# A fused attention and FFN kernel: its hand-kept order of 1,427 work items is replaced by another order

## The chip, the cores and the metric

The kernel runs on one core of a Trainium2 chip. The metric is the device time of one execution in microseconds (us). The engines are TensorE (PE; its weight loads are told as PEld), VectorE (DVE), ScalarE (ACT), GpSimd (POOL) and SyncE (SP). SP only issues transfers here; POOL issues the loads that cast from float32 to bfloat16 on their way, and computes as well. Each engine takes its own instructions in the order in which they were written.

## The reference

```python
def _attn_ref(q, k, v, w_phi):          # q, k, v: (8, 8, 576, 64); w_phi: (64, 128)
    def phi(x):
        proj = np.einsum('bhsd,df->bhsf', x, w_phi)
        proj = proj - np.max(np.abs(proj), axis=-1, keepdims=True)
        return np.concatenate([np.exp(proj), np.exp(-proj)], axis=-1)
    q_p, k_p = (phi(q), phi(k))
    kv = np.einsum('bhsf,bhsd->bhfd', k_p, v)
    z = np.sum(k_p, axis=2)
    num = np.einsum('bhsf,bhfd->bhsd', q_p, kv)
    den = np.einsum('bhsf,bhf->bhs', q_p, z)[..., None] + 1e-06
    return num / den
def _moe_ref(x, w_gate, w_val, w_out):  # x: (4608, 512); d_ff = 1536
    gate = np.maximum(x @ w_gate, 0.0)
    val = x @ w_val
    return gate * val @ w_out
```

The output of the attention, with heads side by side, is x of the FFN. All inputs and the output are float32.

## The kernel before

There are 8 batches of 576 tokens. Of a batch, 512 tokens are one group of the FFN (groups 0 to 7), and the last 64 tokens of all batches ("tails", taken two batches at a time) make group 8. Batches 0 and 1 are turned (tokens to columns) by TensorE; from batch 2 on (`TURN = 2`) k, q and x are turned by DMA, on SP's queue.

The program is cut into 1,427 work items ("atoms"). A planner outside the kernel has put them into one list, the string `ORDER`; the kernel walks the list and lets each atom issue its instructions. An apostrophe behind a number takes the atom's second choice of engine (ACT or DVE for a copy, POOL or DVE for a product). `z5` issues 5 filler matmuls on zeros, which only keep TensorE busy. The list sets the order on each engine and in each queue: an instruction that must wait holds up all that stands behind it on its engine. What waits for what follows from the tiles. PSUM is a ring of 8 banks, so a matmul group also waits for the readers of the bank eight allocations ahead of it.

Atoms are named here by their kind and place, with batch, item, half and so on behind it:

- `ld.k6`, `ld.q1`, `ld.v4`, `ld.wv1`, `ld.km3`, `ld.qm0`: loads. Those of k, q and the weights cast and are issued by POOL (`L214`, `L220`, `L236`, `L243`); those of v are float32 and are issued by SP. `km`, `qm` and `vm` are the tails. A batch's k, q and tails have one buffer each, v has two.
- `turn.k.2`, `turn.qm.0`: turns of k, q or tails by DMA from SP (`L292`, `L298`). `xd.3.2`: the turn of the third quarter of x of batch 3 by DMA from SP (`L639`), into `xT`; batch "8" there is the tails.
- Work on k: `kT`, `kTc` (turn on PE and its copy, `L271`, `L284`; batches 0 and 1), `kr` (projection, PE, `L312`), `km` (row maxima, DVE, `L319`), `ke` (two exponentials, ACT, `L368`), `kk` (exponentials of the maxima, ACT, `L379`), `vs` (v times these, POOL or DVE, `L328`, `L410`), `kv` (PE, `L482`; `L505` for batches 0 and 1, 72 matmuls), `kvc` (its copy, `L418`).
- Work on q: `qT`, `qTc`, `qr`, `qm`, `qc` (PE, `L543`), `qe` (ACT, `L561`), `qk` (ACT, `L577`), `n` (PE, `L591`), `nt` and `nu` (DVE, `L610`, `L622`), `xu` (reciprocal on DVE, product on POOL, `L629`, `L631`), then `xd`, or for batches 0 and 1 `xT` and its copy `xc` (`L651`).
- FFN: `fv`, `fg` (four matmuls each, `L721`; the copy of `fv` is `L736`, the product of `fg` `L743`), `fo` (four matmuls, `L769`; every third one also copies and stores its result, `L783`, `L750`).

The loads of k and v of batch 0 and the constants stand ahead of the list and are the same in both kernels.

Of the kernel before, what the change touches and what calls it, by code (L numbers as in the profile page):

```python
# [22 lines left out]

ORDER = """z5 92 82 83' 93 7 94 97 102 84 98 88 8 95 99 0 103 85 87 89 86 104 105 96 112 107 109 122 113 123
108 114 115 106 117 124 127 100 90 132 133 101 91 110 126 125 119 118 128 111 z3 148 129 149 116
187 188 134 135 137 151 156 153 155 158 120 121 142 144' 160 143' 1 139 10 138 246 247 150 131 196
198 154 130 157 159 152 161 141 136 200 140 29 175 190 189 194 162 176 193 192 163 164 145 147' 195
191 236 165 177 2 146 169 199 170 166 167 181 171 178 168 321 179 201 172 182 217 197 180 237' 322'  # L30
183 184 220 266 267' 282 9 218 214 215 3 221 219 222 4 216 223 256 257' 173 174' 226 208 185 186
209 54 283' 202 203 238 242 210 205 206 227 204 207 211 1092 241 1093 240 1094 1095 1096 1097 224
225' 239 1098 212 213' 324 326 228 229 232 5 1099 231 1100 11 39 230 328 1101 1102 233 1103 1104'
1105 1106 1107 234 258 268 269 262 259 270 260 271 273 261 263 6 272 248 249 275 251 253 255 243
1108 1109 1110 1111 1112' 1113 250 252 1114 1115 284 254 288 330 334 264 286 361 365 332 274 1116
1117 335 290 292 363 265 279 280' 323 325 285 327 289 1118' 1119 287 294 245 235 1120 244 291 293
295 281 276 360 329 277 331 278 296 1121 13 1122' 30 1123 333 31 14 303 304 1124 342 305 300 301
# [3 lines left out]
1134 358 359' 398 401 402 58 61 388 1135 1136 392 389 60 1137 1138 32 391 399 403 59 63 1139 414  # L41
415 1140' 400 1141 367 368 1142 390 1143 15 393 42 373 369 374 375 62 1144 1145 1146 1147 384 1148
419 421 395 64 418 394 422 425 427 429 1149 1150 423 396 397 430 1151 420 17 43 454 458 456 424 385
426 386 387' 416 417' 404 405 406 428 459 407 463 460 462 464 461 465 453 65 431 432 433 1152 437
438 445 446 457 1153 455 434 435 436 1154' 448 449 1155 439 440 441 1156 450 447 442 1157 443 444
472 473 451 452 33 1158' 469 470 483 477 478 1159 1160 466 479 1161 1162 1163 484 485 480 534 471
467 468 474 475 481 476 508 482 486 538 498 501 20 487 509 536 376 1164 1165' 502 1166 511 535 537
539 529 533 500 513 510 512 1167 1168 1169 518 522 499 515 519 531 528 564 568 503 520 1170 530 505
52 55 504 521 18 514 540 1171 1172' 566 1173 569 488 492 489 1174' 491 573 1175 493 494 532 523 524
1176' 377 495 1177 1178' 516 571 1179 1180' 490 496 497 517 570 66 69 563 565 506 567 1181 1182 34  # L50
# [4 lines left out]
585 1200 616 586 617 646 650 618 657 23 647 661 620 649 651 653 1201' 659 648 1202 1203 608 1204  # L55
1205 691 609 610 626 627 695 693 619 621 21 629 631 628 22 46 56 663 665 623 630 667 1206 633 1207
1208' 1209 642 1210' 662 666 656 692 694 696 658 660 622 664 1211 1212' 644 645' 624 625 632 634
635' 698 702 697 701 699 736 739 1213 672 700 652 1214 1215 1216 1217 654 668 740 718 673 737 669
670 703 671 738 741 742 655 1218' 1219 1220 675 707 676 721 614 722 674 680 677 1221 1222 715 678
681 682 679 708 709 1223 723 615 716 717 1224 686 719 720 687 688 1225 1226 1227 1228 683 684 746  # L60
749 724 748 756 685 747 758 766 1229 768 1230' 1231 704 705 1232 706 760 36 710 711 1233 689 47 750
757 690 770 751 752 712 759 725 713 714 1234 802 804 743 726 728 773 730 727 761 762 729 777 775
1235 1236 25 1237 1238 1239 806 767 771 26 769 731 772 774 801 53 805 776 1240' 778 49 1241 753 754
755' 803 1242 837 841 807 809 733 732 808 810 1243' 1244' 811 744 763 764 745 765 734 735 24 1245
785 779 812 782 783 784 780 781 839 813 1246 1247 796 1248' 814 815 1249 37 820 821 822 816 1250
1251 786 787 817 818 819 823 824 1252 1253 1254 74 797 78 798 836 788 75 840 1255 838 1256' 76 1257
77 790 791 48 792 1258 846 842 847 825 826 828 1259 1260' 829 830 848 827 789 1261 1262 793 831 832
794 795 1263 849 850 851 1264 1265 1266 1267 1268 864 38 833 834 835 866 854 858 884 885 886 867
865 799 856 800 1269 1270' 1271 1272 868 1273 1274 857 855 859 874 869 887 870 877 900 902 878 876
79 894 80 1275 1276 1277 896 1278 875 860 1279' 1280' 898 1281 888 843 904 844 879 881 845 1282  # L70
1283 901 27 903 895 899 861 929 897 931 1284' 1285 933 1286 905 1287 930 889 964 966 932 967 935
939 965 937 968 871 1288' 872 880 882 883 28 50 873' 934 890 1289 862 863 891 892 893' 994 936 940
938 906 941 974 977 1290 1291 907 908 909 975 996 1292 1293 978 910 911 912 979 980 976 995 913 914
852 969 970 915 916 1294 57 997 1295 1296 998 921 853 917 956 957 922 999 1001 918 919 942 943 958
1297 1298 1299 1300 923 944 924 925 926 948 81 949 950 1301 1302' 1303 920 945 946 947 951 952 1000
1304 984 988 927 928 1046 1048 971 987 1004 1006 1305 953 1306 1307 1050 959 985 989 960 1002 1003
1008 1308 954 955 986 961 962 963 1309' 1310 972 973' 1005 1009 1007 981 1010 1014 1012 1040 1044
1042 1311 1312 1051 1039 1011 1043 1045 1047 1013 982 1313 983' 1041 1314 1315' 1316' 1317 1318
1028 1015 1016 1029 1052 1053 1054 1034 1035 1036 1058 1059 1049 1060 991 1319 1320 1321 990 1322
1323 1324 1325 992 993' 1030 1326' 1327 1069 1070 1063 1064 1071 1031 1328' 1329 1065 1055 1056  # L80
# [6 lines left out]
1404 1405 1406 1407 1408 1409 1410 1411 1412 1413 1414 1415 1416 1417 1418 1419 1420' 1421 1422  # L87
1423 1424 1425 1426'"""


class Atoms:
# [28 lines left out]
def kernel(  # L120
# [690 lines left out]

    atoms.run(ORDER, keep_busy)
# [28 lines left out]
```

## Time and profile before

| | us |
|---|---|
| median of 3 runs | 383.99 |
| lowest, highest | 382.81, 384.39 |
| profiled execution | 383.07 |
| its span | 381.3 |
| TensorE busy | 366.9 |
| VectorE busy | 280.2 |
| ScalarE busy | 221.9 |
| GpSimd busy | 153.4 |

The span runs from the first to the last instruction of the profiled execution; the time of the execution has 1.8 us more. Busy times are sums over the span. They hide where an engine waits, so they have to be read by stretches: the attention of batches 0 and 1 fills the first 32 us, from there to about 310 us the attention of one batch runs beside the FFN of earlier ones, and the FFN of the last groups fills the rest.

### The profile page before, as it was taken

How to read it: one execution, taken by the hardware profiler on the slowest of the kernel's cores; microseconds unless marked ns; L12 is line 12 of the kernel's file. 1: busy time of each engine (PE TensorE's matmuls, PEld its weight loads, DVE VectorE, ACT ScalarE, POOL GpSimd, SP SyncE). 2: the span in 40 equal slices, each digit the busy share in tenths (PEclk: the TensorE clock that was granted, in tenths of full speed). 3: DMA queues.
4: the chain of work that ended last, by engine and by line, in shares of the span. 5: the costliest groups of instructions: out<-in, count | busy, mean ns of one | idle time of the engine just before them, and what ended most of it. 6: DMA issues, size and time to landing. Idle time of an engine off the chain costs nothing.

```text
span 381.3 us, 8930 instructions
## 1 busy us (share of the span) xinstructions
PE 366.9 (96%) x3454; PEld 199.0 (52%) x3504; DVE 280.2 (73%) x617; ACT 221.9 (58%) x521; POOL 153.4 (40%) x203
## 2 busy tenths in 40 slices
PE   6979999999999999899999999999999999999996
PEld 3658555546544655365546454555555444444443
DVE  6889888888988799779877984999767905845421
ACT  5889887788388657774972549783751413200221
POOL 5856672568356365713680314816800400100000
PEclk9989999999999999999999999999999999999999
DMA  7999999799399827961698903671310150001004
GB/s 238 233 232 165 179 177 161 185 209 204 70 134 254 100 55 133 221 141 34 85 166 164 214 15 107 152 114 29 98 55 2 28 113 28 15 36 74 2 2 108
DMA packets 87929, 45.10 MB, mean 118 GB/s; under 512 B 55824, under 2 KB 82000, under 8 KB 87888
## 3 DMA queue, kind: packets, MB, share of 16 engines
q1 hardware_dynamic: 60208, 30.42, 35.0%
q0 software_dynamic: 27200, 13.57, 29.0%
q10 hardware_dynamic: 480, 0.56, 0.6%
q8 instruction: 27, 0.44, 0.5%
q14 instruction: 14, 0.11, 0.1%
HBM read 37.78 MB, written 9.44 MB: 124 GB/s over the span
## 4 chain that ended last, share of the span: by engine, by line
PE 88%; DMA 4%; ACT 3%; issue 2%; DVE 1%; POOL 1%; SPq 0%; DVEq 0%; POOLq 0%
PE pa L721 49%; PE pa L769 22%; PE pa L591 5%; PE pa L312 4%; PE pa L482 4%; PE pa L543 2%; DMA xT<-xu 2%; DMA vn<-in_k_dram 2%; ACT kp L368 1%; PE pa L505 1%; PE pa L271 1%; ACT qp L561 1%; ACT tT L284 1%; SPq L220 0%; POOL xu L631 0%
## 5 line engine op out<-in xcount | busy, mean ns | idle before, releaser
L743 DVE SCALAR_TENSOR_TENSOR h<-pa,val_sb 128x512 bf16<-128x512 f32 (+1 forms) x112 | 74.4, 669 | 35.0 <-PE pa L721 30.1
L721 PE MATMUL pa<-xT,wv_sb 128*128 128x512 bf16 (+1 forms) x384 | 97.8, 370 | 2.1 <-DMA xT<-xu 1.0
L721 PE MATMUL pa<-xT,wg_sb 128*128 128x512 bf16 (+1 forms) x384 | 98.0, 370 | 0.8
L769 PE MATMUL pa<-wo_sb,h 128*128 128x512 bf16 (+2 forms) x428 | 96.9, 373 | 1.5 <-issue 1.0
L736 ACT CAST val_sb<-pa 128x512 bf16<-128x512 f32 (+1 forms) x75 | 42.8, 575 | 85.5 <-PE pa L721 82.7
L328 POOL TENSOR_TENSOR vs<-vn,ek 128x512 bf16<-128x512 f32 (+1 forms) x70 | 69.3, 1000 | 44.6 <-ACT ek L379 39.9
L561 ACT ACTIVATE qp<-pa 128x512 bf16<-128x512 f32 x144 | 75.7, 619 | 16.8 <-PE pa L543 14.6
L368 ACT ACTIVATE kp<-pa 128x512 bf16<-128x512 f32 (+1 forms) x152 | 77.6, 601 | 12.2 <-PE pa L312 10.4
L631 POOL TENSOR_TENSOR xu<-u,r 128x512 bf16<-128x512 f32 x36 | 37.4, 1043 | 115.1 <-DVE r L629 79.5
L721 PEld LDWEIGHTS <-wv_sb 128*128 128x128 bf16 x448 | 41.5, 98 | 45.0 <-PE pa L769 1.5
L769 PEld LDWEIGHTS <-h 128*128 128x128 bf16 x444 | 41.0, 98 | 45.7 <-issue 1.1
L721 PEld LDWEIGHTS <-wg_sb 128*128 128x128 bf16 x448 | 41.4, 98 | 43.4 <-issue 0.7
L319 DVE TENSOR_REDUCE mk<-pa 128x4 f32<-128x512 f32 (+1 forms) x76 | 47.4, 651 | 8.3 <-PE pa L312 4.2
L319 DVE TENSOR_REDUCE mq<-pa 128x4 f32<-128x512 f32 x72 | 46.6, 681 | 3.3 <-PE pa L312 2.9
L610 DVE TENSOR_TENSOR t<-pa,cq 128x195 f32<-128x195 f32 (+3 forms) x120 | 37.8, 328 | 4.1 <-PE pa L591 3.1
L622 DVE TENSOR_TENSOR u<-pa,t 128x195 f32<-128x195 f32 (+3 forms) x120 | 38.1, 332 | 3.4
L591 PEld LDWEIGHTS <-qp 128*128 128x128 bf16 x640 | 28.4, 98 | 14.0 <-issue 0.9
L736 DVE CAST val_sb<-pa 128x512 bf16<-128x512 f32 (+1 forms) x37 | 25.1, 678 | 12.0 <-PE pa L721 11.2
L591 PE MATMUL pa<-kv,qp 128*128 128x65 bf16 x640 | 31.1, 194 | 0.4 <-ACT qp L561 0.2
L783 ACT COPY out_sb<-pa 128x512 f32<-128x512 f32 (+1 forms) x22 | 13.1, 594 | 26.2 <-PE pa L769 25.8
L783 DVE COPY out_sb<-pa 128x512 f32<-128x512 f32 x14 | 9.6, 687 | 21.0 <-PE pa L769 20.8
L482 PEld LDWEIGHTS <-kp 128*128 128x128 bf16 x480 | 16.5, 98 | 3.6 <-issue 0.8
(66 smaller groups left out, 265.8 us busy)
## 6 DMA issues: line engine op xcount, KB each, us to landing
out_dram<-out_sb SPq DMA_DIRECT2D x32, 256.0 KB, 2.5
vn<-in_v_dram SPq DMA_DIRECT2D x6, 1024.0 KB, 7.8
qn<-in_q_dram POOLq DMA_DIRECT2D x8, 512.0 KB, 8.8
kn<-in_k_dram POOLq DMA_DIRECT2D x6, 512.0 KB, 8.6
wv_sb<-in_moe_w_val_dram POOLq DMA_DIRECT2D x3, 512.0 KB, 10.1
wg_sb<-in_moe_w_gate_dram POOLq DMA_DIRECT2D x3, 512.0 KB, 8.8
wo_sb<-in_moe_w_out_dram POOLq DMA_DIRECT2D x1, 1536.0 KB, 14.7
vn<-in_v_dram SPq DMA_DIRECT2D x1, 1152.0 KB, 10.4
```

Of the source, the lines that this page charges most:

```text
L319: nc.vector.tensor_reduce(m, some.rearrange("p (c f) -> p c f", f=F), axis=AX.X, op=ALU.max, apply_absolute_value=True,)
L328: eng.tensor_tensor(dst[:, :, s, 0:D], src, ek[:, :, s : s + 1].to_broadcast(list(src.shape)), op=ALU.mult,)
L368: nc.scalar.activation(st["kp"][:, s, 0 : n // 2, par, :], st["banks"][par][:, 0 : n // 2 * F].rearrange("p (a f) -> p a f", f=F), AF.Exp, ...
L561: nc.scalar.activation(x["qp"][:, s, slot].rearrange("p a b -> p (a b)"), st["cols", i][par], AF.Exp, scale=sign,)
L591: nc.tensor.matmul(pn[:, E * (2 * i + s) : E * (2 * i + s + 1)], lhsT=x["qp"][:, s, slot, blk, :], rhs=kv_of(b, lo + i)[:, s, :],)
L610: nc.vector.tensor_tensor(x["t", j][rows, 0:n], ab[:, :, 1], c[:, :, None].to_broadcast([np_, n, E]), op=ALU.mult,)
L622: nc.vector.tensor_tensor(x["u"][rows, lo : lo + n], ab[:, :, 0], x["t", j][rows, 0:n], op=ALU.add)
L631: copy_of(alt, nc.gpsimd, nc.vector).tensor_tensor(x["xu"], x["u"][:, :, 0:D], x["r"].to_broadcast([P, H, D]), op=ALU.mult)
L721: nc.tensor.matmul(ps, lhsT=w[:, dc, P * fi : P * fi + P], rhs=xTs[g][:, dc, lo:hi], start=(dc == 0), stop=(dc == NDC - 1),)
L736: copy_by(copy_of(alt, "ACT", "DVE"))(st["val", n], ps)
L743: nc.vector.scalar_tensor_tensor(st["h2"][:, fi, lo:hi], ps, 0.0, st["val", n], op0=ALU.max, op1=ALU.mult)
L769: nc.tensor.matmul(po, lhsT=st["h2"][:, fi, P * t : P * t + P], rhs=wo_sb[:, fi, c0:c1], start=(fi == 0), stop=(fi == NFC - 1),)
```

## The change

Only `ORDER` is replaced. The atoms, their code and their number are the same; both lists hold each of them once. Filler matmuls go from `z5` and `z3` to `z3` and `z1`. Two atoms of `vs` go from POOL to DVE. Of the copies, 14 `kvc` on DVE become 15, 37 `fv` become 33, 15 `fo` become 14; 4 `kTc` on ACT become 7, 2 `qTc` become 1, 6 `xc` become 5. All else is place. The words of the change say that the planner now charges an order for transfers that other transfers push back, and keeps the turns of x by DMA clear of casting loads.

The diff is too long to show whole (some 63 lines out and in). Its head, and the lines that hold the last turn of x for batch 3 (atom 586) and the load of k for batch 6 (atom 23):

```diff
-ORDER = """z5 92 82 83' 93 7 94 97 102 84 98 88 8 95 99 0 103 85 87 89 86 104 105 96 112 107 109 122 113 123
-108 114 115 106 117 124 127 100 90 132 133 101 91 110 126 125 119 118 128 111 z3 148 129 149 116
-187 188 134 135 137 151 156 153 155 158 120 121 142 144' 160 143' 1 139 10 138 246 247 150 131 196
...
-585 1200 616 586 617 646 650 618 657 23 647 661 620 649 651 653 1201' 659 648 1202 1203 608 1204
...
+ORDER = """7 z3 82 83' 92 93' 84 88 87 85 8 94 98 96 97 89 91' 95 102 103' 0 z1 104 105 99 107 112 122 113 114
+86 106 109 108 123 124 90' 117 116 128 1 132 100 115 148 110 125 119 133' 127 118 101 187 134 111
+120 121 129 149 151 188 131 10 126 155 153 156 160 246 130 157 142 137 158 135 139 141 247' 159 161
...
+1193 1194 584 1195 1196 605 604 611 34 606 607 576 1197 638 577 643 578 585 586 1198 1199 1200 657
...
+725 675 676 709 677 672 673 1224 1225 674 1226 683 684 685 746 766 749 756 757 23 770 678 679 750
...
```

Places in the two lists (counted from 0) of atoms that the text speaks of:

| atom | number | before | after |
|---|---|---|---|
| `vs.0.0.1`, on POOL before, on DVE after | 91 | 42 | 16 |
| `km.0.1.0` | 95 | 13 | 17 |
| `kk.0.1` | 99 | 14 | 24 |
| `ld.q1` | 10 | 73 | 62 |
| `ld.wv1` | 2 | 109 | 86 |
| `ld.qm0` | 29 | 91 | 99 |
| `turn.qm.0` | 54 | 156 | 100 |
| `ld.v1` | 9 | 136 | 107 |
| `qT.1.1`, the first user of `ld.q1` | 321 | 120 | 141 |
| `xT.0.1`, `xc.0.1` (on DVE before, on ACT after) | 185, 186 | 153, 154 | 149, 155 |
| `fv.0.0`, the first step of the FFN | 1092 | 169 | 171 |
| `vs.1.0.0`, the first user of `ld.v1` | 234 | 204 | 200 |
| `xd.2.2` | 476 | 513 | 531 |
| `ld.v4` | 18 | 560 | 545 |
| `fv.2.0` | 1172 | 564 | 579 |
| `ld.km3` | 36 | 855 | 650 |
| `xd.3.2` | 586 | 702 | 694 |
| `ld.k6` | 23 | 708 | 836 |
| `xd.4.0` | 679 | 817 | 839 |
| `ld.q5` | 22 | 736 | 744 |
| `fv.3.0` | 1208 | 747 | 739 |

More of the change, by code (lines that the diff above doesn't have):

```diff
@@ L22 @@
 LAST = ((0, 352), (352, 512))
-ORDER = """z5 92 82 83' 93 7 94 97 102 84 98 88 8 95 99 0 103 85 87 89 86 104 105 96 112 107 109 122 113 123
-108 114 115 106 117 124 127 100 90 132 133 101 91 110 126 125 119 118 128 111 z3 148 129 149 116
-187 188 134 135 137 151 156 153 155 158 120 121 142 144' 160 143' 1 139 10 138 246 247 150 131 196
-198 154 130 157 159 152 161 141 136 200 140 29 175 190 189 194 162 176 193 192 163 164 145 147' 195
-191 236 165 177 2 146 169 199 170 166 167 181 171 178 168 321 179 201 172 182 217 197 180 237' 322'
@@ L31 @@
[L31 to L36, printed above, removed]
@@ L37 @@
-295 281 276 360 329 277 331 278 296 1121 13 1122' 30 1123 333 31 14 303 304 1124 342 305 300 301
[3 rows of a table removed]
[L41 to L50, printed above, removed]
[4 rows of a table removed]
@@ L55 @@
-585 1200 616 586 617 646 650 618 657 23 647 661 620 649 651 653 1201' 659 648 1202 1203 608 1204
[L56 to L77, printed above, removed]
@@ L78 @@
-1042 1311 1312 1051 1039 1011 1043 1045 1047 1013 982 1313 983' 1041 1314 1315' 1316' 1317 1318
-1028 1015 1016 1029 1052 1053 1054 1034 1035 1036 1058 1059 1049 1060 991 1319 1320 1321 990 1322
-1323 1324 1325 992 993' 1030 1326' 1327 1069 1070 1063 1064 1071 1031 1328' 1329 1065 1055 1056
[6 rows of a table removed]
-1404 1405 1406 1407 1408 1409 1410 1411 1412 1413 1414 1415 1416 1417 1418 1419 1420' 1421 1422
-1423 1424 1425 1426'"""
+ORDER = """7 z3 82 83' 92 93' 84 88 87 85 8 94 98 96 97 89 91' 95 102 103' 0 z1 104 105 99 107 112 122 113 114
@@ new lines @@
+86 106 109 108 123 124 90' 117 116 128 1 132 100 115 148 110 125 119 133' 127 118 101 187 134 111
+120 121 129 149 151 188 131 10 126 155 153 156 160 246 130 157 142 137 158 135 139 141 247' 159 161
+136 150 143' 152 144' 190 2 192 194 236 237 140 154 196 256 138 163 198 200 29 54 162 175 257' 176
+164 165 9 189 191 201 3 145 147' 146 177 266 267 166 167 169 195 170 168 171 181 182 4 172 178 179
+183 180 193 226 184 199 214 215 197 216 321 322' 217 282 220 218 173 174' 185 11 283 5 202 219 186'
@@ new lines @@
+221 203 222 208 209 204 223 238 205 206 227' 207 240 210 211 1092 1093 1094 1095 1096 39 224 239
+225' 1097 241 228 232 324 212 213 229 1098 1099 242 231 6 230 326 328 1100 1101 1102 233 234 1103
+1104 1105 1106 1107 268 271 243 272 270 30 258 259 260 51 269 261 273 275 248 249 262 251 253 1108'
+274 263 1109 1110 1111 1112 265 264 252 1113 1114 250 1115 1116 1117 290 292 361 365 255 254 279
+363 294 281' 291 295 280' 13 244 323 327 293 1118 1119 325 284 286 330 332 334 235 245 276 278 277'
+288 285 289 329 331 333 1120' 1121 1122 287 296 1123 315 335 297 298 312 313 300 301 302 14 342 343
[6 rows of a table added]
@@ new lines @@
+463 1152 509 15 386 387' 395 405 406 407' 453 457 427 430 394 396 397 1153 1154' 510 512 445 431
+434 432 433 513 1155 446 455 442 443 444 414 415 416 417 447 1156 437 438 439 465 477 435 436 440
+1157 478 1158' 1159 469 441 65 480 481 479 482 448 449 450 483 484 485 486 1160 52 1161 1162 518
+487 498 522 472 1163 451 452 499 501 500 466 467 473 470 502 474 471 503 468 475 1164 1165 476 521
+515 1166 520 519 534 536 523 564 566 524 538 529 18 533 531 525 505 1167 1168 1169 568 19 528 532
+569 573 535 539 537 571 530 1170 1171' 570 540 488 489 492 574 526 572 575 527' 490 491 493 1172'
@@ new lines @@
+1173 32 55 1174 1175 20 1176 44 1177 1178 514 516 494 517 504 506 507 547 548 66 69 67 495 563 565
+549 567 496 497' 376 68 555 1179 544 545 546 1180 1181 541 542 587 1182 543 588 558 589 550 551
[4 rows of a table added]
+21 1204' 1205 72 1206 691 693 626 663 667 622 627 695 630 665 1207' 1208' 628 629 1209 1210 22 1211
+656 631 46 660 658 662 664 692 696 694 623 652 633 1212' 1213 1214' 666 632 634 635 624 625 736 697
+701 698 737 738 1215 1216' 1217 56 653 654 655 715 702 699 700 739 644 721 669 645 703 614 722 723
+716 717 668 1218 1219 1220' 670 1221 671 718 719 615 377 1222 740 707 708 720 724 704 705 706 1223
@@ new lines @@
+725 675 676 709 677 672 673 1224 1225 674 1226 683 684 685 746 766 749 756 757 23 770 678 679 750
+758 759 741 743 1227 1228 1229 1230 686 687 688 760 680 681 682 1231 710 1232 1233 53 773 802 711
+712 713 714 689 768 761 806 763 762 726 729 727 728 731 733 1234' 1235 690 730 1236 742 777 1237
[3 rows of a table added]
+799 800 1250' 1251 1252 1253 1254 26 831 1255 1256 832 828 829 830 825 78 826 827 833 834 1257 1258
[3 rows of a table added]
+902 1275 1276' 1277 1278 876 904 866 890 843 844 1279' 877 1280' 845 878 1281 1282 879 880 1283 929
+931 901 903 860 895 933 897 1284 905 861 1285 1286 899 28 1287 891 906 930 934 964 881 965 968 935
@@ new lines @@
+939 937 967 872 1288 1289 873' 966 932 1290 1291 1292 1293 882 883 994 997 852 974 996 50 978 853
[5 rows of a table added]
+1042 1039 1045 973 1007 1043 1011 1015 1002 1003' 1315' 992 993' 1034 1316' 1317 1318' 1047 1319
[5 rows of a table added]
+1355 1356 1357 1358' 1359 1360 1361 1362 1363 1364' 1365 1366' 1367 1368 1369 1370 1081 1082 1083
+1090 1091 1371 1372 1373 1374 1375 1376 1377 1378' 1379 1380 1381 1382 1383 1384 1385 1386 1387
+1388 1389 1390' 1391 1392' 1393 1394 1395 1396 1397 1398' 1399 1400' 1401 1402' 1403 1404' 1405
+1406' 1407 1408' 1409 1410' 1411 1412 1413 1414 1415 1416 1417 1418 1419 1420 1421 1422 1423 1424
@@ L91 @@
+1425 1426'"""
 class Atoms:
```

38 rows, old and new, of the table ORDER are left out of this document.

## The prediction

> **What bounds the kernel now.** I read the page first, then the busy time by stretches, then the chain of waits, and then the timelines of the two places where TensorE stands idle. The page:
>
> ```profile
> span 381.3 us, 8930 instructions
> ...
> PE 366.9 (96%) x3454; PEld 199.0 (52%) x3504; DVE 280.2 (73%) x617; ACT 221.9 (58%) x521; POOL 153.4 (40%) x203
> ...
> PE 88%; DMA 4%; ACT 3%; issue 2%; DVE 1%; POOL 1%; SPq 0%; DVEq 0%; POOLq 0%
> ```
>
> TensorE (PE) is busy 96% of the span, and 88% of the chain that ended last is its own work. A new order of the same matmuls can win only what PE loses by waiting: 381.3 - 366.9 = 14.4 us at the most by this line. Where that is shows in stretches (columns: length, then busy us and instructions of PE, PEld, DVE, ACT, POOL, granted clock, DMA share, GB/s):
>
> ```profile
> 0.00:32.00 32.00, 25.55 (x377) 17.38 (x378) 24.32 (x60) 24.99 (x65) 22.19 (x39) 0.95 1.11 222
> 32.00:116.00 84.00, 83.05 (x926) 47.90 (x940) 71.87 (x164) 65.52 (x159) 47.55 (x62) 1.00 1.05 170
> 116.00:148.00 32.00, 31.74 (x321) 17.40 (x323) 26.56 (x63) 21.37 (x52) 17.53 (x23) 1.00 0.80 127
> 148.00:160.00 12.00, 10.64 (x94) 5.28 (x94) 9.75 (x19) 9.77 (x24) 7.33 (x11) 1.00 0.94 169
> 160.00:370.00 210.00, 208.26 (x1697) 106.90 (x1725) 146.63 (x312) 98.73 (x221) 58.77 (x71) 1.00 0.40 79
> 370.00:381.30 11.30, 7.63 (x48) 4.12 (x45) 1.01 (x2) 1.50 (x3) 0.00 (x0) 0.98 0.35 93
> ```
>
> PE's idle time is 32 - 25.55 = 6.5 us in the start, 1.36 us in 148 to 160, 3.67 us at the end (the last output and its store, which the new order leaves as they are, but for one copy that changes its engine), and in the other 326 us only 0.95 + 0.26 + 1.74 = 2.95 us. So there are three things to price: one stall, the start, and whether the dense 326 us stay dense.
>
> **The change, part by part.** No operation is added. Four of the eight filler matmuls at the start go, and two products of v go from POOL to VectorE; all else is place in the list and which engine copies.
>
> *The stall at 157 us goes: -1.3 us.* The chain, in order of time (start, us, what), with PE's pace in the dense part:
>
> ```profile
> 149.64 7.69 DMA xT<-xu
> ...
> 346.52 9.28 PE pa L721 x43
> ```
>
> PE's timeline, POOL's, and the page's list of DMA issues (median us to landing last):
>
> ```profile
> 157.58 1.02 PE L721 MATMUL pa<-xT,wv_sb 128*128 128x512 bf16 x4 [1.04 <-DMA xT<-xu]
> ```
>
> ```profile
> 149.56 0.95 POOL L214 DMA_DIRECT2D kn<-in_k_dram  x1
> ```
>
> ```profile
> xT<-xu SPq DMA_TRANSPOSE x24, 2.7
> ```
>
> The last turn of x for batch 3 (xd.3.2) was issued at 149.64, 0.08 us behind the casting load of k for batch 6 (ld.k6). It took 7.69 us, where the median is 2.7, and the FFN of batch 3 waited for it. The new order has xd.3.2 at place 694; the nearest casting loads in the list are ld.km3, 44 places ahead, and ld.q5, 50 behind; ld.k6 is now at 836. Between xd.3.2 and the first FFN step of batch 3 (fv.3.0) PE has ten output steps instead of seven. A step is 4 matmuls of 9.28 / 43 = 0.216 us, so 0.86 us, and three steps are 2.6 us, more than the wait. I take the whole excess of that stretch: 1.36 less the 0.1 us that 12 us lose elsewhere. The Trainium skill, DMA: Bandwidth & Descriptors, section Queues, rings and completion order, says that a DMA engine goes round between the queues that have work, packet by packet. By that a turn beside one load would take at most about twice its 2.7 us and this stall would not have been there, so the sum would be 1.3 us higher; the 7.69 us row speaks against it, and the measurement decides.
>
> *The start: +0.8 us, between +0.2 and +2.7.* The start ends when the first FFN step (fv.0.0) begins, at 31.97. ScalarE (ACT) is the engine with the fewest gaps there, so I follow it. Rows of the timeline of the first 36 us:
>
> ```profile
> 5.37 0.75 DVE L319 TENSOR_REDUCE mk<-pa 128x2 f32<-128x256 f32 x2 [0.49 <-PE pa L312]
> ...
> 5.83 0.66 ACT L368 ACTIVATE kp<-pa 128x256 bf16<-128x256 f32 x2 [0.58 <-DVE mk L319]
> ...
> 7.95 1.77 POOL L328 TENSOR_TENSOR vs<-vn,ek 128x256 bf16<-128x256 f32 x3 [0.24 <-DMA vn<-in_v_dram]
> ...
> 12.53 1.08 ACT L368 ACTIVATE kp<-pa 128x512 bf16<-128x512 f32 x2 [1.07 <-PE pa L312]
> ...
> 13.50 0.31 ACT L379 ACTIVATE ek<-mk 128x8 f32<-128x8 f32 x2
> ...
> 13.69 2.06 ACT L368 ACTIVATE kp<-pa 128x512 bf16<-128x512 f32 x4
> ...
> 16.75 2.12 ACT L561 ACTIVATE qp<-pa 128x512 bf16<-128x512 f32 x4
> ...
> 24.72 0.38 ACT L418 CAST kv<-pa 128x260 bf16<-128x260 f32 x1 [0.56 <-PE pa L505]
> ...
> 27.22 0.61 ACT L284 COPY tT<-pa 128x512 bf16<-128x512 bf16 x1
> ...
> 27.99 0.45 PEld L271 LDWEIGHTS <-qn 128*128 128x128 bf16 x8 [1.70 <-DMA qn<-in_q_dram]
> ...
> 28.65 1.86 ACT L284 COPY tT<-pa 128x1024 bf16<-128x1024 bf16 x3 [0.83 <-PE pa L271]
> ...
> 30.41 0.59 ACT L651 COPY xT<-pa 128x512 bf16<-128x512 bf16 x1
> 30.89 1.03 ACT L284 COPY tT<-pa 128x1024 bf16<-128x1024 bf16 x1
> ```
>
> ```profile
> 31.97 0.60 PE L721 MATMUL pa<-xT,wv_sb 128*128 128x256 bf16 x4 [0.21 <-ACT tT L284]
> ```
>
> The new order puts vs.0.0.1 on VectorE (DVE) ahead of km.0.1.0, and it needs the v load that lands at 7.9. DVE waits, multiplies (0.4 us, as two 256-wide reductions take 0.75; a copy of 0.15) and reduces (0.4) until 8.9, so ACT cannot start kk.0.1 before 9.0. Then follow, in the list, kk 0.31, ke.0.0.0 0.66, ke.0.2.0 1.03, kk 0.31, ke.0.2.1 1.03: 12.4. From there to the copy of x that fv.0.0 needs (xc.0.1, now on ACT) the list gives ACT 4 wide ke (4 x 1.03), 2 narrow (2 x 0.66), 8 qe (8 x 1.06), 3 kk and 2 qk (5 x 0.31), copies of 0.4 (half of 0.61, and its fixed part), 2 x 0.61, 1.03, 0.38 and 2 x 0.59: 19.7 us, so 32.1, and the FFN at 32.2. That is +0.2 with no gap at all, the lower end. Before, ACT had gaps of 1.07, 0.56 and 0.83 in this stretch; all of them again would make it +2.7, the upper end. I keep the 0.56 (the copy of kv still stands ahead of three qe), and drop the rest: the 0.83 came from the q of batch 1, which landed late, and its load is now 11 places earlier with its use 21 places later. That makes +0.8.
>
> *The load of v for batch 1: nothing.* In the new order turn.qm.0 stands ahead of ld.v1 on SyncE's (SP) queue, and it waits for the q tails, which POOL loads behind one weight load more. SP takes in order, so v waits too. The row of that turn before, the page's row of the load, and POOL's first use:
>
> ```profile
> 28.94 1.31 SPq L298 DMA_TRANSPOSE qmT<-qm  x1
> ```
>
> ```profile
> vn<-in_v_dram SPq DMA_DIRECT2D x1, 1152.0 KB, 10.4
> ```
>
> ```profile
> 39.11 1.04 POOL L328 TENSOR_TENSOR vs<-vn,ek 128x512 bf16<-128x512 f32 x1 [2.68 <-ACT ek L379]
> ```
>
> If the tails land when they did, v is issued at 30.6 and lands at 41, 2 us after POOL would use it. POOL has 36 us free of 84 in that stretch, which hides it; with no cover it would cost those 2 us. Behind turn.qm.0 and ld.v1 on SP stands only the turn of k for batch 2, whose user is over 20 us of PE work away. Against it stands that 1.15 MB less is moved while the DMA share is 1.11; I count neither.
>
> *The dense part: +0.3 us, between -1.5 and +1.5.* Ahead of fv.2.0 the new list has two ke, three qe, two km and three qm more: 5 x 1.05 = 5.3 us more for ACT, 5 x 0.7 = 3.5 us for DVE, in a stretch where they have 84 - 65.52 = 18.5 and 12.1 us free. It fits, with less slack; I charge a third of the 0.95 us that PE loses there. The ends are half of the 2.95 us, won or lost.
>
> **Sum.** The profiled execution took 383.07 us (span 381.3 and 1.8 around it), 0.92 us less than the median of 383.99. 383.07 - 1.3 + 0.8 + 0.3 = 382.9; on the median's scale 383.8. That is no change: about 0.5% (1.9 us) is what a measurement of this kernel can tell from none.
>
> **Rivals.** *The clock stays low through the start (slower).* These rows are the same 72 matmuls at two times, and the granted clock (last but two) from 22 to 26:
>
> ```profile
> 16.70 1.52 PE L505 MATMUL pa<-vs,kp 64*128 64x65 bf16 x72
> ...
> 22.43 2.27 PE L505 MATMUL pa<-vs,kp 64*128 64x65 bf16 x72
> ```
>
> ```profile
> 22.00:24.00 2.00, 1.84 (x60) 1.75 (x62) 2.00 (x5) 2.00 (x6) 1.24 (x2) 0.60 1.28 216
> 24.00:26.00 2.00, 2.00 (x44) 1.53 (x39) 1.28 (x5) 1.35 (x4) 0.00 (x0) 0.54 1.45 195
> ```
>
> At half clock (1.6 + 1.8 us by these two rows) the group takes 0.75 us longer. The three filler matmuls that stood at 12.7 us are gone from there; one stands some 7 us earlier. If the clock then stays at half until the FFN runs, two such groups cost 1.5 us and one more 3.4 us stretch at half rate, now of FFN steps, 1.7: 3.2 on top of the sum, 387.0. It decides when half clock reaches beyond some 32 us. For it: the clock already fell once in this start. Against it: it came back while PE did no more than this work. The Trainium skill, TensorE: Matmul & The Clock Gate, Part 1, says that the clock opens after about 3.4 us of sustained activity and closes after an idle window, and so speaks against taking filler out; the 3.4 us of these rows agree.
>
> *Another transfer is late instead (the turns are not clear).* xd.2.2 is now followed on SP by the 1 MB load ld.v4, 14 places on, with 6 output steps and some attention work up to fv.2.0; xd.4.0 still stands 3 places behind ld.k6, but 19 us of PE work ahead of its use. If xd.2.2 takes 7.69 us again, the old 1.3 us are back and a bit more, say 1.7: 385.5. For it: 7.69 us came out of such a neighbourhood. Against: this load casts nothing.
>
> *The dense part gets denser (faster).* Start at its lower end and half of the 2.95 us won: 383.07 - 1.3 + 0.2 - 1.5 + 0.9 = 381.4. For it: a wait priced in the list is a wait avoided. Against: the extra early work for DVE and ACT.
>
> **How the numbers follow.** The forecast's case 0.44, the clock 0.2, the other transfer 0.18, the denser part 0.18. Faster by over 0.5% (below 382.1): most of the last and little of the first, 0.18. Slower (above 385.9): most of the clock's, a good third of the transfer's and a bit of the first, 0.30. Within: 0.52. The range goes from the faster rival to the clock's price: 381.2 to 387.0; the forecast's own is 382.3 to 385.6.
>
> **What would show it.** Right: no wait of PE for xT of 1 us at fv.3.0, the turn before it landing in under 4 us; fv.0.0 at 32 to 33.5; ACT's first wait near 7.6 to 9 us for DVE, DVE's for vn at 7.9; v of batch 1 issued near 30. Wrong: PE's idle time between 32 and 370 over 5 us, fv.0.0 after 35 us, or a granted clock below 1 beyond 32 us.

## The result, and the profile after

The new order takes 381.09 us (median of 7 runs, 380.42 to 382.63), the old one beside it 384.86 (7 runs, 382.81 to 386.37): a ratio of 0.9912, 95% interval 0.9884 to 0.994. Some executions of a list take over 1.5% longer than its fastest one; the ratios here and below leave these out. The new order is faster by 0.9%, where I had forecast no change: 381.09 us lies just below the 381.2 at which my range ended. The profiled execution took 381.09 us, its span is 379.3, 2.0 less than before.

The page of the new order:

```profile
span 379.3 us, 8924 instructions
...
PE 366.2 (97%) x3450; PEld 198.3 (52%) x3500; DVE 279.7 (74%) x615; ACT 223.7 (59%) x526; POOL 152.7 (40%) x200
...
PE 91%; DMA 3%; ACT 2%; issue 1%; POOL 1%; DVE 1%; SPq 0%; DVEq 0%
```

TensorE's busy time fell by 0.7 us and its idle time, 379.3 - 366.2, by 1.3. By stretches (columns as in the prediction):

```profile
0.00:32.00 32.00, 25.76 (x388) 17.74 (x389) 25.96 (x66) 27.11 (x71) 23.30 (x39) 0.89 1.22 217
32.00:116.00 84.00, 82.96 (x939) 47.14 (x950) 71.57 (x162) 66.12 (x162) 45.84 (x60) 1.00 0.98 172
116.00:148.00 32.00, 31.74 (x319) 17.35 (x321) 25.07 (x62) 19.29 (x46) 15.80 (x20) 1.00 0.87 130
148.00:160.00 12.00, 11.89 (x97) 5.75 (x94) 10.88 (x20) 10.35 (x25) 9.65 (x13) 1.00 0.88 209
160.00:370.00 210.00, 208.21 (x1687) 107.11 (x1716) 145.92 (x307) 99.24 (x223) 58.11 (x72) 1.00 0.37 77
```

The stall went: 148 to 160 us is idle for 0.11 us, before for 1.36. The dense 326 us show 1.04 + 0.26 + 1.79 = 3.09 us of idle time, before 2.95. The first 32 us hide their change: TensorE is as busy as before, at a mean clock of 0.89 where it was 0.95, and yet gets further. PE's timeline has the first FFN step (fv.0.0) and the first of batch 3 (fv.3.0):

```profile
30.22 0.60 PE L721 MATMUL pa<-xT,wv_sb 128*128 128x256 bf16 x4
...
155.57 0.81 PE L721 MATMUL pa<-xT,wv_sb 128*128 128x512 bf16 x3
```

The FFN begins at 30.22, not at 31.97, and fv.3.0 waits for nothing. The start is where I was wrong. Why it is shorter shows in the load of q for batch 1 (`ld.q1`, POOL's timeline), and in the weight loads of TensorE that use it (PEld):

```profile
16.17 0.95 POOL L214 DMA_DIRECT2D qn<-in_q_dram  x1
```

```profile
26.10 0.46 PEld L271 LDWEIGHTS <-qn 128*128 128x128 bf16 x8
```

The load by itself, from issue to landing, after:

```profile
DMA to landing us min/median/max: 8.3/8.3/8.3
```

and before, where it was issued at 16.72:

```profile
DMA to landing us min/median/max: 11.2/11.2/11.2
```

It now lands at 24.5 and nobody waits for it; before it landed at 27.9 and TensorE had waited 1.70 us. What had moved beside it was the 1.15 MB load of v for batch 1, which is now issued behind the turn of the q tails (SP's timeline):

```profile
27.95 1.30 SPq L298 DMA_TRANSPOSE qmT<-qm  x1
29.49 0.40 SPq L220 DMA_DIRECT2D vn<-in_v_dram  x1
...
147.33 1.20 SPq L639 DMA_TRANSPOSE xT<-xu  x1
```

### The profile page after: what moved, and what is told of

The parts are those of the page before. It is cut to its first block, busy times and chain, and to the rows that moved or that the text cites. A ratio compares the mean times of both kernels' runs of the same rounds, so it can differ in the third digit from the quotient of the medians.

```text
span 379.3 us, 8924 instructions
## 1 busy us (share of the span) xinstructions
PE 366.2 (97%) x3450; PEld 198.3 (52%) x3500; DVE 279.7 (74%) x615; ACT 223.7 (59%) x526; POOL 152.7 (40%) x200
## 3 DMA queue, kind: packets, MB, share of 16 engines
q1 hardware_dynamic: 60208, 30.42, 33.5%
## 4 chain that ended last, share of the span: by engine, by line
PE 91%; DMA 3%; ACT 2%; issue 1%; POOL 1%; DVE 1%; SPq 0%; DVEq 0%
PE pa L721 49%; PE pa L769 24%; PE pa L591 5%; PE pa L312 4%; PE pa L482 4%; DMA kn<-in_k_dram 3%; PE pa L543 2%; ACT qp L561 2%; PE pa L505 1%; DMA vn<-in_k_dram 1%; PE pa L271 1%; POOL xu L631 1%; SPq L220 0%; DVE u L622 0%; DVE t L610 0%
## 5 line engine op out<-in xcount | busy, mean ns | idle before, releaser
L736 ACT CAST val_sb<-pa 128x512 bf16<-128x512 f32 (+1 forms) x79 | 45.0, 574 | 69.7 <-PE pa L721 69.3
L328 POOL TENSOR_TENSOR vs<-vn,ek 128x512 bf16<-128x512 f32 (+1 forms) x68 | 68.1, 1014 | 36.3 <-DMA vn<-in_v_dram 16.2
L769 PEld LDWEIGHTS <-h 128*128 128x128 bf16 x444 | 40.7, 98 | 44.4 <-issue 1.2
L736 DVE CAST val_sb<-pa 128x512 bf16<-128x512 f32 x33 | 22.7, 687 | 3.3 <-PE pa L721 2.8
L482 PE MATMUL pa<-vs,kp 128*128 128x65 bf16 x384 | 17.5, 193 | 0.1
## 6 DMA issues: line engine op xcount, KB each, us to landing
vn<-in_v_dram SPq DMA_DIRECT2D x1, 1152.0 KB, 11.2
```

Source lines behind the costliest of these rows:

```text
L328: eng.tensor_tensor(dst[:, :, s, 0:D], src, ek[:, :, s : s + 1].to_broadcast(list(src.shape)), op=ALU.mult,)
L482: nc.tensor.matmul(kv_ps[:, hh, s, :], lhsT=lhsT, rhs=rhs, start=(n == 0), stop=(n == 19))
L736: copy_by(copy_of(alt, "ACT", "DVE"))(st["val", n], ps)
L769: nc.tensor.matmul(po, lhsT=st["h2"][:, fi, P * t : P * t + P], rhs=wo_sb[:, fi, c0:c1], start=(fi == 0), stop=(fi == NFC - 1),)
```

## The experiments

The theory: the start is shorter because `ld.v1` no longer moves beside `ld.q1`, and the stall is gone because `ld.k6` no longer stands beside xd.3.2. The rivals: it is the new order of the matmuls and copies in the start, the filler, or the denser rest. Ratios are to the old list run beside each. For the profiles I use two numbers: when fv.0.0 starts, and what is left of the span from there, which prices all that follows the start. Each run has one profile, of one of its executions.

**The new start, then the old rest (start_new).** The first 171 items as in the new list, all others behind them in the order of the old one.

```diff
-ORDER = """z5 92 82 83' 93 7 94 97 102 84 ... 207 211 1092 241 [the old rest]
+ORDER = """7 z3 82 83' 92 93' 84 88 87 85 ... 210 211 242 1092 241 [the old rest]
```

> The new list up to the first FFN step, then the old list for all that is left. Theory A (the gain is the vanished stall at the FFN of batch 3 and the rest of the list; the start itself gains nothing by order, and began sooner in the new profile only because the first loads landed 2 us sooner): about the old time, ratio 0.998 to 1.003, and the wait of PE for xT of about 1 us near 157 us is still there. Theory B (the start gains by its order): 1.5 us less, ratio about 0.996. In both the first load pieces of k and v land as it happens in that execution; fv.0.0 starts at 30.2 if they land by 7.3 us, near 32 if by 9.3.

Measured: 382.71 us (381.24 to 391.78), ratio 0.9953 (0.9926 to 0.998). fv.0.0 started at 30.48. The profiled execution took 388.16 us and shows a wait that the new list does not have:

```profile
62.87 1.04 PE L769 MATMUL pa<-wo_sb,h 128*128 128x512 bf16 x4 [4.38 <-DMA wo_sb<-in_moe_w_out_dram]
```

The load of the output weights was issued at 40.33 in this mixture and at 32.9 in the new list. No trace shows whether the shorter executions, on which the ratio rests, have this wait too. So the new start brings time with the old rest as well, 0.2 to 0.7% by the interval, and how much the mixture loses by a wait of its own stays open. The load of k still stands beside xd.3.2 here, and that turn took 7.9 us.

**The old start, then the new rest (start_old).** The reverse.

```diff
-ORDER = """7 z3 82 83' 92 93' 84 88 87 85 ... 210 211 1092 [the new rest]
+ORDER = """z5 92 82 83' 93 7 94 97 102 84 ... 5 240 1092 [the new rest]
```

> The old list up to the first FFN step, then the new list. Theory A: nearly the whole gain, ratio 0.991 to 0.994 (381 to 382 us on the chip where the old one takes 384). Theory B: what is left without the start, ratio 0.995 to 0.997. No wait for xT at the FFN of batch 3 in either.

Measured: 383.87 us (383.26 to 385.44), ratio 0.9985 (0.9969 to 1.0002). PE's timeline, and the stretch of the old stall:

```profile
32.74 0.60 PE L721 MATMUL pa<-xT,wv_sb 128*128 128x256 bf16 x4 [0.22 <-ACT tT L284]
```

```profile
148.00:160.00 12.00, 11.90 (x99) 5.89 (x100) 10.13 (x22) 9.05 (x22) 10.68 (x13) 1.00 0.68 182
```

The stall is gone, but the new rest brings 0.6 us (1.2 to none by the interval), where removing the stall alone brings 1.0 (next experiment). These intervals overlap. The profiles point the same way: 348.9 us follow fv.0.0 here and 348.4 there, so the rest gives something back.

**Only the load of k is moved (old_k6_late).** In the old list `ld.k6` goes from place 708 to behind fg.3.1.

```diff
-... 646 650 618 657 23 647 661 620 ... 660 622 664 1211 1212' 644 ...
+... 646 650 618 657 647 661 620 ... 660 622 664 1211 23 1212' 644 ...
```

> The old list with one atom moved: the casting load of k for batch 6 from 6 places behind the last turn of x for batch 3 to behind the second FFN step of that batch. If the load beside it is what held the turn, the turn lands in under 4 us and the kernel takes 1.3 to 1.7 us less, ratio 0.9955 to 0.997. If the turn is late for another reason (the store or SP's queue), it still takes over 6 us and the ratio is 0.999 to 1.001.

Measured: 383.55 us (382.79 to 393.54), ratio 0.9973 (0.996 to 0.9987), 1.0 us less. xd.3.2 was issued at 151.0 and landed 2.4 us later; the stretch of the stall:

```profile
148.00:160.00 12.00, 11.68 (x100) 5.89 (x100) 10.73 (x23) 9.61 (x24) 5.51 (x9) 1.00 0.65 117
```

Its start is that of the old list, with a wait of TensorE's weight loads for the q of batch 1 twice as long as in the profile of before:

```profile
28.38 0.45 PEld L271 LDWEIGHTS <-qn 128*128 128x128 bf16 x8 [3.56 <-DMA qn<-in_q_dram]
```

One moved load makes the turn quick, and it is worth about 1 us. The twelve profiles of this case agree without exception: the turn took 7.6 to 7.9 us in the four lists that have this load beside it (old, old_v1_late, start_new, new_k6_near) and 2.4 to 2.5 us in the other eight.

**The load of k back beside the turn, in the new list (new_k6_near).** This asks whether the clear turn matters there, or the greater distance to its user covers it.

```diff
-... 577 643 578 585 586 1198 1199 1200 ... 749 756 757 23 770 678 ...
+... 577 643 578 585 23 586 1198 1199 1200 ... 749 756 757 770 678 ...
```

> The new list with the same load put right ahead of the last turn of x for batch 3, as close as the old list had it. If the new list gains by keeping the load clear of the turn: the turn takes 6 to 8 us again. With ten output steps behind it, 10.6 us of PE work, that still is hidden, so within 0.3 us of the new list, ratio 0.991 to 0.993; if clearness itself is what counts, 1.3 us more, ratio about 0.995.

Measured: 383.03 us (382.07 to 388.85), ratio 0.9955 (0.994 to 0.997). The span is 381.2 with fv.0.0 at 30.38, so 350.8 us follow, 1.7 more than in the new list. SP's timeline, and the turn from issue to landing:

```profile
147.50 1.21 SPq L639 DMA_TRANSPOSE xT<-xu  x1
148.84 0.50 SPq L750 DMA_DIRECT2D out_dram<-out_sb  x1
```

```profile
DMA to landing us min/median/max: 7.6/7.6/7.6
```

The turn, 2.5 us in the new list, was slow again and landed at 155.1. TensorE would have come to it at about 155.9 and lost nothing. But the store behind it took 7.7 us where it takes 2.3 in the new list, and this came of it on DVE and PE:

```profile
156.78 0.69 DVE L783 COPY out_sb<-pa 128x512 f32<-128x512 f32 x1 [3.08 <-DMA out_dram<-out_sb]
```

```profile
157.53 0.81 PE L721 MATMUL pa<-xT,wv_sb 128*128 128x512 bf16 x3 [1.63 <-DVE out_sb L783]
```

VectorE waited 3.08 us for the output buffer that the store still read, and TensorE 1.63 us for the PSUM bank that VectorE had not emptied. The cover that I had counted on does hide the turn, and the loss comes back through the store. Keeping the casting load away is what gains here, not the distance.

**The load of v early again, in the new list (new_v1_first).** `ld.v1` goes ahead of turn.qm.0.

```diff
-... 163 198 200 29 54 162 175 257' 176 164 165 9 189 191 ...
+... 163 198 200 29 9 54 162 175 257' 176 164 165 189 191 ...
```

> The new list with one atom moved: the load of v for batch 1 goes ahead of the turn of the q tails of batches 0 and 1 on SP's queue, so that it is issued near 13 us, as in the old list, and not near 29.5. Theory C (the start gains because this load no longer runs beside the load of q for batch 1): q of batch 1 lands near 27 and not at 24.4, the first FFN step starts 1 to 2 us later, at 31.5 to 32, and the ratio goes from 0.991 to 0.995 or so. Theory D (the start gains by its order of copies and matmuls on ACT, DVE and PE): the first FFN step stays at 30.2 to 30.5 and the ratio at 0.991 to 0.992.

SP's timeline, the load of q from issue to landing, its user on PEld, and PE:

```profile
12.90 0.38 SPq L220 DMA_DIRECT2D vn<-in_v_dram  x1
```

```profile
DMA to landing us min/median/max: 11.3/11.3/11.3
```

```profile
28.21 0.45 PEld L271 LDWEIGHTS <-qn 128*128 128x128 bf16 x8 [1.05 <-DMA qn<-in_q_dram]
```

```profile
31.49 0.60 PE L721 MATMUL pa<-xT,wv_sb 128*128 128x256 bf16 x4
```

In the profile most of the gain of the start is gone: q takes 11.3 us again and the FFN begins 1.3 us later. Not all of that comes from the load of v. In this execution the first loads landed later (the last 7.6 us after issue, 6.0 in the profile of the new list), and `ld.q1` was issued at 16.89 and not at 16.17. The profiled execution took 382.36 us, the longest of its six runs. The median, 381.66 us (381.39 to 382.36), and the ratio, 0.9929 (0.9914 to 0.9944), do not differ from those of the new list run again (below). The slower q is shown by this profile. A loss of time is not shown: in the new list an early load of v costs nothing that the median can tell.

**The load of v late, in the old list (old_v1_late).** The other direction: `ld.v1` goes from place 136 to behind turn.qm.0, and nothing else.

```diff
-... 220 266 267' 282 9 218 214 215 ... 185 186 209 54 283' 202 ...
+... 220 266 267' 282 218 214 215 ... 185 186 209 54 9 283' 202 ...
```

> The old list with one atom moved: the load of v for batch 1 goes behind the turn of the q tails, so that it is issued near 29 us and not near 13. Theory C: q of batch 1 lands near 25, the first FFN step starts at 30 to 31 and not at 31.7 to 33.3, ratio 0.994 to 0.996, unless the load of the output weights, which then has more beside it, comes too late for its first user near 59 us. Theory D: no change at the start, ratio 0.999 to 1.001.

Measured: 380.74 us (379.92 to 383.51), ratio 0.9916 (0.9889 to 0.9943). SP's timeline, the load of q, and PE:

```profile
28.27 0.39 SPq L220 DMA_DIRECT2D vn<-in_v_dram  x1
```

```profile
DMA to landing us min/median/max: 9.1/9.1/9.1
```

```profile
30.99 0.60 PE L721 MATMUL pa<-xT,wv_sb 128*128 128x256 bf16 x4 [0.22 <-ACT tT L284]
```

This is the cleanest pair of profiles. POOL issued q at 16.72 before and at 16.71 here, and the last of the first loads landed 8.5 and 8.3 us after issue. With v out of the way q took 2.1 us less and the FFN began 1.0 us earlier.

By the ratio, one moved item out of 1,427 gives as much as the whole new list, and it still has the old stall: TensorE waited 1.09 us for the turn, and 349.3 us follow fv.0.0, as before. But the ratio is worth 3.2 us and the profiles show 1.0 of them. The profiled execution took 382.14 us, 1.4 more than the median, and no trace shows where the others gain more.

**The new list with the old filler (new_filler8).** `z5` and `z3` at the places that correspond to those of the old list.

```diff
-ORDER = """7 z3 82 83' 92 ... 102 103' 0 z1 104 105 ... 132 100 115 148 ...
+ORDER = """z5 7 82 83' 92 ... 102 103' 0 104 105 ... 132 100 115 z3 148 ...
```

> The new list with the filler matmuls of the old one (5 at the head and 3 ahead of the turn of q of batch 0 on PE, in place of 3 and 1). If the clock's half-rate stretch of the start (12 to 21 us in the new list) is a cost, it is shorter or gone and the first FFN step is up to 1 us earlier, ratio 0.988 to 0.990. If PE has time to spare there, within 0.5 us, ratio 0.990 to 0.993.

Measured: 381.69 us (380.5 to 383.0), ratio 0.9929 (0.9907 to 0.995). The first stretch, and PE's timeline:

```profile
0.00:32.00 32.00, 25.71 (x395) 17.45 (x396) 25.84 (x66) 27.09 (x71) 23.72 (x39) 1.00 1.17 215
```

```profile
29.91 0.60 PE L721 MATMUL pa<-xT,wv_sb 128*128 128x256 bf16 x4
...
49.66 1.27 PE L505 MATMUL pa<-vs,kp 64*128 64x65 bf16 x72 [1.03 <-POOL vs L328]
```

The clock stays full all through the start, and the FFN begins 0.3 us earlier than in the profile of the new list. The filler is not shown to be the cause of either. start_new and new_start_two_moves (below) have the filler and the start of the new list, and in their profiles the clock is full as well, with the FFN at 30.48 and 30.00. The new list itself had 6.8 us at half clock (rows further below), new_again and new_k6_near as much, and began the FFN at 30.22, 30.57 and 30.38. So half clock comes and goes from execution to execution, and 0.3 us lie within the spread.

The earlier start brings nothing in the end: at 49.66, where the new list has no wait, TensorE waited 1.03 us. v of batch 1 had landed at 41.4 and POOL's products came late. Behind the shorter start stands the load that was put off to make it.

**The new start with three moves in the old rest (new_start_two_moves).** The list of start_new with the load of k late, as in old_k6_late, and the load of the output weights ahead of fv.0.4, which takes away the wait of start_new.

```diff
-... 1099 231 1100 39 ... 261 263 6 272 ... 618 657 23 647 ... 1211 1212' ...
+... 1099 231 6 1100 39 ... 261 263 272 ... 618 657 647 ... 1211 23 1212' ...
```

> The new list up to the first FFN step, then the old list with two atoms moved: the load of k for batch 6 behind the second FFN step of batch 3, and the load of the output weights ahead of the fifth FFN step of batch 0 (in the earlier run of new start and old rest it was issued at 40 us, took 21 us, and PE waited 4.4 us for it). If start and these two transfers are all that matters, it takes what the new list takes or somewhat less, because the old list loses about 1 us less between 32 and 150 us: ratio 0.988 to 0.991. If the rest of the new list gains elsewhere too, 0.992 to 0.995.

Measured: 381.65 us (380.72 to 382.14), ratio 0.9922 (0.9904 to 0.9941). fv.0.0 began at 30.00, and TensorE then waited 1.51 us at the same matmuls, for POOL's work on v (v was issued at 30.70 and landed 13.2 us later). It is no faster than the new list.

**Two moved loads in the old list (old_two_moves).** `ld.v1` as in old_v1_late and `ld.k6` as in old_k6_late, in one list.

```diff
-... 267' 282 9 218 ... 209 54 283' ... 618 657 23 647 ... 664 1211 1212' ...
+... 267' 282 218 ... 209 54 9 283' ... 618 657 647 ... 664 1211 23 1212' ...
```

> The old list with both single moves: the load of v for batch 1 behind the turn of the q tails (alone: ratio 0.9916) and the load of k for batch 6 behind the second FFN step of batch 3 (alone: 0.9973). If the two costs are separate, they add: ratio 0.988 to 0.990, q of batch 1 lands near 25.5 us and no wait at the FFN of batch 3; that is below the new list. If the moved loads only push the loss on to another transfer, 0.991 to 0.993.

Measured: 381.03 us (379.76 to 381.81), ratio 0.9901 (0.9875 to 0.9927). PE's timeline:

```profile
31.01 0.60 PE L721 MATMUL pa<-xT,wv_sb 128*128 128x256 bf16 x4 [0.22 <-ACT tT L284]
...
155.41 1.03 PE L721 MATMUL pa<-xT,wv_sb 128*128 128x512 bf16 x4
```

q was 8.2 us on its way, and no wait is left at fv.3.0. **The new list once more, beside it (new_again):**

> The new list unchanged, on the same chip as the old list with its two moves. If two loads explain the change, it takes 0.990 to 0.992 of the old one and is 0 to 1 us slower than the old list with two moves, because it loses about 0.6 us more between the start and the FFN of batch 3. If the rest of the new order gains elsewhere, it is faster than the old list with two moves.

Measured: 381.59 us (380.63 to 385.88), ratio 0.9933 (0.991 to 0.9957). The old list with two loads moved is as fast as the new one, perhaps faster; the intervals overlap.

The profiles together, in us. The load of q is that of batch 1, from issue to landing; the last column is the span less the start of fv.0.0.

| list | load of q | fv.0.0 | what follows |
|---|---|---|---|
| old | 11.2 | 31.97 | 349.3 |
| old_k6_late | 12.0 | 33.32 | 348.4 |
| start_old | 11.9 | 32.74 | 348.9 |
| new_v1_first | 11.3 | 31.49 | 349.1 |
| old_v1_late | 9.1 | 30.99 | 349.3 |
| old_two_moves | 8.2 | 31.01 | 348.4 |
| new | 8.3 | 30.22 | 349.1 |
| new_again | 8.1 | 30.57 | 349.0 |
| new_k6_near | 8.0 | 30.38 | 350.8 |
| new_filler8 | 7.7 | 29.91 | 349.9 |
| new_start_two_moves | 8.1 | 30.00 | 350.2 |

With v beside it, q takes 11.2 to 12.0 us and the FFN begins at 31.49 or later; without, 7.7 to 9.1 us and 31.01 or earlier. No list of the table breaks this, nor does start_new (7.6 and 30.48).

The rival, the new order of matmuls and copies in the start, is not nothing either. With v out of the way the old start reaches fv.0.0 at 30.99 and 31.01, the new one with its own filler at 30.00 to 30.57 (start_new included): 0.4 to 1.0 us earlier. Which of its moves bring this, no run separates.

## Where the prediction held and where it failed, by its steps

I had given no change a chance of 0.52 and a time below 382.1 us one of 0.18, and the measured time is 381.09. Of the signs that I had named for being right, the quick turn, fv.3.0 without a wait and the issue of v near 30 came; fv.0.0 at 32 to 33.5 and VectorE's wait for v did not.

*The stall, -1.3.* Right in size: its stretch lost 1.25 us of idle time, and removing it alone gave 1.0 us (0.5 to 1.5 by the interval of old_k6_late). My reason was half wrong. I let three more output steps cover a slow turn; new_k6_near has that cover and still lost 1.63 us, through the store queued behind the turn. I followed the turn's user and not the transfer next in the queue, which was slow as well. Whether the load held that store or the turn ahead of it did, no run separates.

For the turn I had weighed the Trainium skill, DMA: Bandwidth & Descriptors, section Queues, rings and completion order, where a DMA engine goes round between queues packet by packet. I read that as about twice the time. The turn took 7.6 us instead of 2.5 beside the load of k, and the store 7.7 instead of 2.3, three times as long. That section of the Trainium skill speaks of packets and not of equal shares in time; no run here shows single packets, and the three times are what decides.

*The start, +0.8 forecast, -1.75 measured.* This is the step that failed, in two ways. The first is the term that I named and left at zero, the 1.15 MB that are no longer moved beside the load of q. I had dropped the 0.83 us gap behind the late q, but because its load stands 11 places earlier. That made its issue 0.55 us earlier; its landing came 3.4 us earlier. The term could have been bounded: 1152 KB at the 222 GB/s of that stretch are 5.3 us of transfer, against 1.70 us that TensorE waited for q. In the old list the later start of `ld.v1` gave 2.1 to 3.8 us in the transfer of q and 1.0 to 2.3 us in the start of the FFN (30.99 and 31.01 against 31.97, 32.74 and 33.32); the clean pair has 2.1 and 1.0. The other 0.8 us of the 1.75 lie between 31.0 and 30.22, and go with the new order of the start. Before's profile also had the earliest start of the three with the old start, so its rows showed the wait at its smallest.

The second is the sum of ACT's work, which was to give a floor of 32.1 us and was too long by some 2.5 us. Even new_v1_first, with q late again, began the FFN at 31.49, below that floor. The new start on ACT:

```profile
7.52 0.30 ACT L379 ACTIVATE ek<-mk 128x4 f32<-128x4 f32 x2 [0.42 <-DVE mk L319]
...
8.52 1.08 ACT L368 ACTIVATE kp<-pa 128x512 bf16<-128x512 f32 x2 [0.15 <-DVE mk L319]
9.49 0.31 ACT L379 ACTIVATE ek<-mk 128x8 f32<-128x8 f32 x2
9.69 3.04 ACT L368 ACTIVATE kp<-pa 128x512 bf16<-128x512 f32 x6
12.56 0.36 ACT L379 ACTIVATE ek<-mk 128x8 f32<-128x8 f32 x2
...
15.85 2.06 ACT L561 ACTIVATE qp<-pa 128x512 bf16<-128x512 f32 x4 [0.52 <-PE pa L543]
...
19.77 2.07 ACT L561 ACTIVATE qp<-pa 128x512 bf16<-128x512 f32 x4 [0.63 <-PE pa L543]
...
24.28 0.38 ACT L418 CAST kv<-pa 128x260 bf16<-128x260 f32 x1 [0.24 <-PE pa L505]
...
28.35 1.30 ACT L651 COPY xT<-pa 128x512 bf16<-128x512 bf16 x2
```

kk.0.1 ran at 7.52, not at 9.0, because the first piece of v was there sooner than in the profile of before: VectorE multiplied it at 6.66, having waited for ACT and not for v. And a row's duration overlaps the next row: the group at 9.69 lasts 3.04 us, but the next starts 2.87 us later, and the 0.31 us at 9.49 cost 0.20. From kk.0.1 to the end of the copies of x I had 23.1 us of work; it took 22.1, to 29.65, and 1.5 of that are the waits in these rows, which leaves 20.6. I added durations where starts should have been subtracted, and so had a floor above what then happened. Nor was ACT the engine that fv.0.0 came behind, as I had it. Its copies of x were done at 29.65, and the chain of the new order that ended last (start, us, what) comes to the FFN through POOL's products of x and then through TensorE's own work:

```profile
27.55 1.04 POOL xu L631
...
28.64 0.40 PE pa L271 x4
...
30.38 2.29 PE pa L721 x20
```

*The load of v, nothing.* Right, with less room than I said: issued at 29.49 (forecast 30.6), landed at 40.7 (41), POOL waited 6.89 us for it and TensorE nothing. new_filler8 and new_start_two_moves show the end of the cover: with the FFN 0.2 to 0.3 us earlier and v 0.7 to 3.2 us later, TensorE lost 1.03 and 1.51 us.

*The dense part, +0.3.* What follows fv.0.0 is 348.4 us in both lists with the old rest and the load of k late, 348.9 to 349.1 in the four with the new rest and no wait of their own: +0.6, within my ends. In the profiles this takes back what the new start has over the old one with v late, so that the new list is not faster than the old one with two moved loads. Which steps lose the 0.6 us, no run shows.

*The rivals.* In the profile of the new order the clock did stay low for longer, as that rival had it, and half clock did not reach the FFN. The granted clock (third column from the right) of the new order:

```profile
14.00:16.00 2.00, 1.77 (x22) 0.81 (x19) 1.89 (x3) 1.48 (x6) 2.00 (x3) 0.59 1.24 208
16.00:18.00 2.00, 1.82 (x44) 1.63 (x46) 1.99 (x6) 2.00 (x7) 1.98 (x4) 0.50 1.23 205
18.00:20.00 2.00, 2.00 (x58) 1.62 (x52) 1.31 (x4) 1.37 (x6) 1.98 (x5) 0.50 1.27 210
20.00:22.00 2.00, 1.88 (x30) 1.30 (x27) 1.91 (x5) 2.00 (x6) 2.00 (x4) 0.71 1.42 193
```

Half clock lasted 1.6 + 2 + 2 + 1.2 = 6.8 us, before 3.4 us. It is cheap here while it ends ahead of the FFN. The same new start reached fv.0.0 at 30.22, 30.57 and 30.38 with 6.8 us of it, and at 30.48 and 30.00 with none. The old start with v late reached it at 30.99 with 10.2 us (old_v1_late, 0.84 in the mean over the first 32) and at 31.01 with 3.4 (old_two_moves). TensorE has time to spare in that stretch: in the new order it is busy for 25.76 of the first 32 us. The other late transfer (xd.2.2 beside the plain load of v) did not come: that turn landed in 2.4 us. The denser dense part, the rival on the right side, came nearest with its 381.4, and by luck: it had +0.2 for the start and -1.5 for the dense part, where the profiles show -1.75 and +0.6.

*The sum.* By the profiles: -1.75 for the start, -0.9 to -1.25 for the stall, +0.6 for the rest, -2.0 in all, against a forecast of -0.2. The medians differ by 3.8 us, 3.4 by the ratio. One reason is that the execution profiled before took 383.07 us, 1.8 less than the median of 384.86, and its start was a good one: with fv.0.0 at 32.74 or 33.32, as in the two other profiles of that start, it would have taken some 383.8 to 384.4 us (my estimate, 349.3 + 1.8 + that start).

*Open:* the rest of that difference, and the 2 us by which old_v1_late gains more in the median than in its profile. The mean granted clock may have a part in it: it was 0.982 to 0.999 in the executions of the old list, and 0.998 or more in five of the six of old_v1_late, the profiled one with 0.986 being the sixth. No trace of those five shows what that is worth. *Open* also: why new_v1_first loses 1.3 us in the profile and nothing in the median. An early v frees POOL of a wait of 6.89 us, but in that profile 349.1 us follow fv.0.0 as in the new list, so it shows nothing given back; that the profiled execution was the longest of its six, with late first loads, fits, and no other trace of that list shows it.

## What to carry to other kernels

Price a transfer that moves out of the way like one that moves in: its bytes at the rate of that stretch bound what it can give to the load beside it (here 5.3 us, of which 2.1 to 3.8 came), and that is a gain only where an engine waits for that load. Where a transfer is slowed by a neighbour, the next one in its queue can be late too, as the store was here, so follow the users of both. Before you take a difference between two profiles for the work of an edit, see how far profiles of one list differ. Make floors from the starts of consecutive instructions and not from the sum of their durations.

## What the runs showed of the hardware

Two executions of the same list can differ in the trace where the chip does the same work: the new list run again shows no idle time of TensorE from 116 to 370 us,

```profile
116.00:148.00 32.00, 32.00 (x320) 17.30 (x316) 25.42 (x63) 19.60 (x46) 15.78 (x20) 1.00 0.86 130
...
160.00:370.00 210.00, 210.00 (x1726) 107.24 (x1723) 146.26 (x308) 99.50 (x223) 58.45 (x72) 1.00 0.36 77
```

where the first profile of it shows 0.11 + 0.26 + 1.79 us, with fewer matmuls recorded (1687 for 1726), and yet 349.0 and 349.1 us follow fv.0.0. Idle time of 1% in a dense stretch is not evidence; the starts of known steps are.

The first loads are issued at the same times in all lists. The last of them landed 8.5 us after issue in the profile of before and 6.1 in start_old, which has the same old start, and between 6.0 and 8.5 in all twelve profiles. The view of start_old:

```profile
DMA to landing us min/median/max: 2.1/3.8/6.1
```

A floor that rests on one such landing has some 2 us of play. And the half clock came in multiples of 3.4 us: 3.4 before, 6.8 after, 6.8 and then 3.4 in old_v1_late, and in old_k6_late 3.4 right behind TensorE's wait of 3.56 us for q. The Trainium skill, TensorE: Matmul & The Clock Gate, Part 1, gives about 3.4 us of sustained activity for the clock to open. The 3.4 us of before agree; the 6.8 us after are twice that, with TensorE busy for 1.77 to 2.00 of every 2 us meanwhile.
